# Four interleaved attention layers on one core: projections of every layer staged through HBM, wider exponentials in the last layer, zeros set later

## The chip, the core and the metric

The kernel runs on one core of a Trainium2 chip. The core has five engines with instruction queues of their own: TensorE (PE, matrix multiplies; PEld is its weight load), VectorE (DVE), ScalarE (ACT), GpSimd (POOL) and SyncE (SP), which here only issues transfers. They meet at semaphores. The metric is the time of one execution in device microseconds; the number to beat is the median of seven runs of the kernel before.

## The reference

Four attention layers follow each other on a sequence of 2048 positions with 640 features, 32 heads of 20 features, all in bf16. Layers 0 and 2 use weights A and a sliding window of 256 keys; layers 1 and 3 use weights B and see all keys.

```
def block(x, wqkv, wo, windowed):
    q, k, v = heads(layernorm(x) @ wqkv)             # 32 heads of 20
    s = (q @ k.T) * 20 ** -0.5
    if windowed: s = where(0 <= i - j < 256, s, -1e9)
    return x + merge(softmax(s) @ v) @ wo
x = block(x, A..., True);  x = block(x, B..., False)
x = block(x, A..., True);  x = block(x, B..., False)
```

No maximum is subtracted in the kernel: it exponentiates the scores, and a column of ones beside V gives the sum to divide by.

## The kernel before

**Tiling.** Queries go in chunks of 512 (`c`, four of them), heads in groups of four (`g`, eight). One `Unit` is a layer, a chunk and a group. A score "bank" holds 128 keys by 512 queries of one head, one of the eight PSUM banks. A full unit has 64 banks (16 key blocks, 4 heads), a windowed one 12. There are 4096 full and 768 windowed banks in all. The four heads of a group lie in four strips of 32 partitions, of which 20 hold data and 12 hold zeros, so that the score matmuls (L889) of different heads run side by side.

**The order.** One Python loop (L866) writes the whole program in order, one "tick" for each tile of three banks (of two for every other tile in the early stage). A tick issues the score matmuls of its tile (L889), the exponential over it on ACT (L903), then side work, then for windowed tiles the mask product on DVE (L935), and last the value matmuls of a tile two or three ticks older (L953), which add up in PSUM bank 7. Score tiles alternate between banks 0 to 2 and 3 to 5; bank 6 (early also 5) is left for the side work. Units of neighbouring layers are interleaved: the first parts of layer 1 run between the windowed units of layer 0, layer 2's windowed units between the units of layer 1 (later 3). The last 24 units are layer 3, chunks 1 to 3, with nothing beside them but their own output projections.

**Side work.** Layer norm (`t_ln`), value, key and query projections (`t_v`, `t_qk_window`, `t_full`), output projection (`t_out`) and the normalization of a finished unit (`t_tail`) are generators in a list sorted by the unit that needs them. `pump` (L220) runs them for as much credit as `rate` (L849) gives the tick: 1.2 before the first full unit, later a value that spreads the work before its due time, at least 0.33 in the last layer; one credit is about 4.5 matmuls of a projection. `chain` gives the early path of layer 0 into layer 1 a lead of five units. `require` runs tasks regardless of credit when a unit cannot be written without them. `keep_clock` (L578) adds matmuls without use (L588) where the side work of the last three ticks is small; it is on from the first full unit up to layer 3, chunk 1.

**Projections.** In layers 1 and 3, `t_full` makes a block of 128 of the 640 columns of K or Q (five matmuls of 128x512), evacuates it into a staging tile (`st`, four of them) and stores it in HBM (`k_d`, `q_d`). `load_unit` (L671) brings a unit's values, keys and queries back: one transfer for V and eight for Q and K, one per strip, all on SP's queue. `load_ahead` issues the next full unit's loads once its blocks are written and buffers are free. In layers 0 and 2, `t_qk_window` makes K and Q of one group directly in SBUF with weights padded from 80 to 128 columns, so each chunk needs eight pairs in place of five. The padded weights are built in layer 0, chunk 0 (`get_w`, L304), kept in HBM (`wqk_d`) and loaded again by later chunks. `cap` lets three query tiles (`qa`) live, so this work can run only three units ahead. Stores of K, Q and V are issued by SP, too.

**The start.** DVE clears `wop`, `kts` and `qts` (L118) and makes small constants (L128 to L139) before the first layer-norm statistics (L356). SP loads the input and the weights meanwhile.

The lines of evacuation are shared: L281 is ACT's copy, L283 DVE's; before the first full unit ACT does them, afterwards DVE.

Of the kernel before, what the change touches and what calls it, by code (L numbers as in the profile page):

```python
# [26 lines left out]
HD = D // 2  # L27
VW = DH + 1

PARTS = {  # L30
# [6 lines left out]
def kernel(  # L37
# [18 lines left out]
    big = pool("big", 1)  # L56
    wqkp = pool("wqkp", 9)
    kvp = pool("kvp", 3)
    qap = pool("qap", 3)
    kap = pool("kap", 18)  # L60
    vap = pool("vap", 10)
# [29 lines left out]
    kts = [big.tile([P, S], BF16, name=f"kt{n}", tag=f"kt{n}") for n in range(3)]  # L91
    qts = [big.tile([P, C], BF16, name=f"qt{n}", tag=f"qt{n}") for n in range(4)]

    ps = psp.tile([P, 8, C], F32, name="ps", tag="ps")
    op = ps[:, 7, :]


    wqk_d = dram.tile([G, P, 2 * KD * P], BF16, name="wqk_d", tag="wqk_d")
    k_d = {l: dram.tile([D, S], BF16, name=f"k_d{l}", tag=f"k_d{l}") for l in (1, 3)}
    q_d = {l: dram.tile([NC, D, C], BF16, name=f"q_d{l}", tag=f"q_d{l}") for l in (1, 3)}  # L100
    v_d = {l: dram.tile([P, G, NT * 4 * VW], BF16, name=f"v_d{l}", tag=f"v_d{l}") for l in (1, 3)}

# [13 lines left out]

    for t in (wop, *kts, *qts):
        nc.vector.memset(t[:], 0.0)  # L118
    nc.gpsimd.memset(ident[:], 0.0)
# [6 lines left out]
    def other_constants():  # L126
        load_wop(0)
        nc.vector.memset(op, 0.0)  # L128
# [48 lines left out]
    def push(name, gen, need, left):  # L177
        lead = 0
        if type(name) is tuple and need <= first_use(1, NC - 1, 0):

            chain = {"out": True, "ln": name[1] == 1, "v": name[1] == 1 and name[-1] == 0}
            chain["k"] = chain["q"] = name[-1] == 0
            lead = 5 * chain.get(name[0], False)
        insort(todo, Task(name, gen, need, left, lead))
# [77 lines left out]
    live = Counter()  # L262
    cap = {"qa": 3, "ka": 18, "va": 10, "xnT": 5, "kt": 3, "vt": 3, "qt": 4, "ln": 1, "w": 4, "vs": 2}

# [26 lines left out]
    def get_w(l, n, c, i):  # L291

        t = wqkp.tile([P, KD, P], BF16, name="wqk", tag="wqk")
        wtick[l, n, c, i] = state["tick"] + 4
        if l % 2:
            a = n * D + i * P
            nc.sync.dma_start(out=t[:], in_=wq_view[1][:, :, a : a + P])
            return t
        d = wqk_d[i][:, n * KD * P : (n + 1) * KD * P]
        if l == 0 and c == 0:  # L300
            tv = t[:].rearrange("p c (j m) -> p c j m", j=4)
            nc.gpsimd.memset(tv[:, :, :, DH:32], 0.0)
            src = raw[:, :, n * D + 80 * i : n * D + 80 * (i + 1)]
            nc.vector.tensor_copy(  # L304
                out=tv[:, :, :, 0:DH], in_=src.rearrange("p c (j e) -> p c j e", j=4)
            )
            nc.sync.dma_start(out=d, in_=t[:].rearrange("p c m -> p (c m)"))
            wtick[l, n, c, i] = 0
        else:
            nc.sync.dma_start(out=t[:].rearrange("p c m -> p (c m)"), in_=d)  # L310
        return t
# [48 lines left out]
    def t_ln(l, c):  # L360
# [3 lines left out]
        for n in (1, 0):  # L364
            order = worder[l, n]
            if order and not any(e in wtiles for e in order):
                wtiles[order[0]] = get_w(*order[0])
        users[l, c] = (9, 12, 9, 11)[l]
        mv = mvs.pop((l, c))
# [35 lines left out]
    def t_v(l, c, halves):  # L405
# [41 lines left out]
        for h in halves:  # L447
            if not windowed:
                nc.sync.dma_start(
                    out=v_d[l][:, 4 * h : 4 * h + 4, c * 16 * VW : (c + 1) * 16 * VW],  # L450
                    in_=vs[h][:].rearrange("p g i e -> p g (i e)"),
                )
                live["vs"] -= 1
            ready.add(("v", l, c, h))
# [8 lines left out]

    def t_qk_window(l, c, g):
        while ("xnT", l, c) not in ready:
            yield ("wait", 1)
        yield from room("qa", "ka", "w", "w")
        wt = yield from take_w(l, 0, c, g)
        q = qap.tile([P, C], BF16, name="qa", tag="qa")
        yield from project(wt, xnT[l, c], lambda: q[:])  # L470
        wt = yield from take_w(l, 1, c, g)
        k = kap.tile([P, C], BF16, name="ka", tag="ka")
        yield from project(wt, xnT[l, c], lambda: k[:])
        live["w"] -= 2
        qa[c, g], ka[c, g] = q, k
        used(l, c)
        ready.add(("qk", l, c, g))

    def t_full(l, n, c, b):

# [6 lines left out]
        dst = k_d[l][rows, c * C : (c + 1) * C] if n else q_d[l][c, rows, :]  # L487
        nc.sync.dma_start(out=dst, in_=staging.pop())
        live["w"] -= 1
# [66 lines left out]
    def push_layer(l, c):  # L556
# [3 lines left out]
        if l % 2:  # L560
            halves = ((0,), (1,)) if l == 1 else ((0, 1),)
            for h in halves:
                push(("v", l, c, *h), t_v(l, c, h), need[4 * h[0]], 2.8 * len(h))
            for b in range(KD):
                g = b * P // 80
                for n in (1, 0):
                    worder[l, n].append((l, n, c, b))
                    first = need[g] if n else index[l, c, g, PARTS[l][0] if c == 0 else None]
                    push(("qk"[n], l, c, b), t_full(l, n, c, b), first, 1.1)
            return  # L570
        for g in range(G):
            for n in (0, 1):
                worder[l, n].append((l, n, c, g))
            push(("qk", l, c, g), t_qk_window(l, c, g), need[g], 2.2)
            if g == 0:
                push(("v", l, c), t_v(l, c, (0, 1)), need[0], 5.6)
# [83 lines left out]
    units += [Unit(3, c, g) for c in range(1, NC) for g in range(G)]  # L660
    full = [u for u in units if not u.windowed]
    place = {id(u): n for n, u in enumerate(full)}
    index = {(u.l, u.c, u.g, u.part): n for n, u in enumerate(units)}

    def first_use(l, c, g):
# [3 lines left out]
        return next(index[l, 0, g, p] for p in PARTS[l] if 4 * c < p[1])  # L669

    def load_unit(u):  # L671

        l, c, g = u.l, u.c, u.g
        key = (l, c, g)
        k0, k1 = key_blocks(l, u.part)
        live["vt"] += 1
# [6 lines left out]
        live["qt"] += 1  # L683
        kt[key] = kts[len(loaded) % 3]
        qt[key] = qts[len(loaded) % 4]
        for j in range(4):
# [6 lines left out]
    def unit_needs(u):  # L693
        l, c, g = u.l, u.c, u.g
        if u.windowed:
            return [("qk", l, c, g)]
        k0, k1 = key_blocks(l, u.part)
        chunks = range(k0 // 4, k1 // 4)
        blocks = range(80 * g // P, (80 * g + 79) // P + 1)
        return [("q", l, c, b) for b in blocks] + [  # L700
            n
# [6 lines left out]
    def ensure_loaded(u, force):  # L708
# [6 lines left out]
        elif any(n not in ready for n in needs) or any(  # L715
            live[t] >= cap[t] for t in ("kt", "vt", "qt")
        ):
            return
# [3 lines left out]
    def start_unit(u):  # L722
        for n in unit_needs(u):
            require(n)
        if not u.windowed:
            ensure_loaded(u, True)

    def load_ahead():

        for u in full:  # L730
            if id(u) not in loaded:
                ensure_loaded(u, False)
                return

# [28 lines left out]
    def s_emitted(u):  # L763
        if u.windowed:
            live["qa"] -= 1
            live["ka"] -= (u.c > 0) + (u.c == NC - 1)
        else:
# [9 lines left out]
    def t_tail(l, c, g, on, oT):  # L777
# [38 lines left out]
        if g == G - 1:  # L816
            need = first_use(l + 1, c, 0) if l < 3 else len(units) + c
            push(("out", l, c), t_out(l, c), need, 9.0)
            if l < 3:
                push_layer(l + 1, c)  # L820
    def t_stats0(c):
        for i in range(4):
# [4 lines left out]
    with tc.manual_schedule():  # L827
        other_constants()
        push("stats", t_stats0(0), 0, 0.4)
        push_layer(0, 0)  # L830
        require(("qk", 0, 0, 0))

# [8 lines left out]
        n = 0  # L841
        while n < len(banks):
            size = 2 if len(tiles) % 2 and narrow(banks[n][0]) else 3
            for b in banks[n : n + size]:
                starts.setdefault(id(b[0]), len(tiles))
            tiles.append(banks[n : n + size])
            n += size

        def rate(t):  # L849

            u = tiles[t][0][0]
            if index[u.l, u.c, u.g, u.part] < woven:
# [7 lines left out]

        last_tick[0] = state["tick"] + len(tiles) - 40
        work = deque(maxlen=3)
        started = set()
        pts = deque()
        pushed = set()
        for t in range(len(tiles) + 8):  # L866
            state["tick"] += 1
            n_b = 0
            if t < len(tiles):
                cur = tiles[t]  # L870
                n_b = len(cur)
                for b in cur:
                    u = b[0]
                    if id(u) not in started:
# [9 lines left out]
                        start_unit(u)  # L884
                sp = ps[:, 0:3, :] if t % 2 == 0 else ps[:, 3:6, :]
                for n in range(2):
# [6 lines left out]
                for b in cur:  # L893
                    if b[-1]:
                        s_emitted(b[0])
                pt = ptp.tile([P, 3, C], BF16, name="pt", tag="pt")
                i = 0
# [21 lines left out]
                state["heat"] = 0.0  # L919
            else:  # L920
                pump(2.0, 2.0)

            if 0 < t <= len(tiles):
                cur_, pt_ = masked
                i = 0
                while i < len(cur_):
# [12 lines left out]
                    i = k  # L939
            if n_b:  # L940
                masked = (cur, pt)

# [54 lines left out]
```

The softmax here doesn't subtract the row's maximum and nothing guards it: scores larger than these inputs give would overflow.

## Time and profile before

| | |
|---|---|
| median of 7 runs | 2438.05 us (2423.5 to 2439.68) |
| profiled execution | 2438.93 us, span 2437.2 us |
| busy | PE 2012.9, ACT 2234.8, DVE 871.3, POOL 39.7 us |
| exponentials (L903) | 1704, 2199.0 us |
| projections of K and Q (L337) | 956 matmuls recorded |
| matmuls without use (L588) | 562 |
| granted TensorE clock, mean | 0.829 of full speed |

The profile lists, for each engine, busy time and idle time with the instruction that ended it. Its views used here are: busy time by stretch of the span (columns: stretch, its length, then busy microseconds and instructions of each engine, the granted clock, the share of DMA time and the rate), the waits of one engine (columns: who waited for whom, total, times, longest), and the instructions in order of time (columns: start, duration, engine, line, operation, tiles, count, and the idle time before with its releaser). Matmuls are pipelined and their ends are modelled, so a PE that reads as busy may still have room.

### The profile page before, as it was taken

The page shows a single profiled execution, that of the slowest core. Times are in us where ns is not written, and L with a number is a line of the kernel's source. Part 1 is how long each engine was busy: PE and PEld are TensorE (multiplying, and loading weights), DVE is VectorE, ACT ScalarE, POOL GpSimd, SP SyncE. Part 2 cuts the span into 40 slices and gives each one's busy share as a digit, 9 for nine tenths or more (in the row PEclk, how much of TensorE's full clock was granted, in tenths as well). Part 3 has the DMA queues.
Part 4 walks back from the last instruction along what each step waited for, and adds up shares of the span by engine and source line. Part 5 has one row for each costly group of instructions (what it writes and reads, how often), then busy time and mean ns, then how long its engine had stood idle before and what let it go on. Part 6 is the DMA issues. An engine that isn't in the chain of part 4 may idle for free.

```text
span 2437.2 us, 38778 instructions
## 1 busy us (share of the span) xinstructions
PE 2012.9 (83%) x15662; PEld 741.5 (30%) x15811; DVE 871.3 (36%) x1966; ACT 2234.8 (92%) x1779; POOL 39.7 (2%) x112
## 2 busy tenths in 40 slices
PE   6889889888888898888888898888777777777777
PEld 2334333323322333323322333332222222222222
DVE  6767767423333244433353434542200010001001
ACT  5778888899899999999998999999999999999997
POOL 1000000000000000000000000000000000000000
PEclk9899999987999999989997999999755575557556
DMA  4213223222100122102320032122100010011100
GB/s 146 60 41 82 65 63 91 56 73 74 47 24 26 39 61 80 41 13 55 82 67 16 16 89 75 31 46 63 57 28 26 25 36 26 25 35 31 34 13 12
DMA packets 141124, 120.19 MB, mean 49 GB/s; under 512 B 66064, under 2 KB 129680, under 8 KB 140944
## 3 DMA queue, kind: packets, MB, share of 16 engines
q1 hardware_dynamic: 140944, 117.70, 18.3%
q8 instruction: 124, 2.03, 0.3%
q14 instruction: 56, 0.46, 0.1%
HBM read 96.40 MB, written 21.23 MB: 48 GB/s over the span
## 4 chain that ended last, share of the span: by engine, by line
ACT 43%; PE 31%; issue 14%; DVE 10%; DMA 1%; SPq 0%; POOL 0%; ACTq 0%; DVEq 0%
ACT pt L903 43%; PE ps L337 7%; PE ps L889 7%; PE ps L953 5%; PE ps L510 4%; DVE pt L935 3%; PE ps L588 3%; PE ps L428 3%; DVE oT L760 1%; PE ps L392 1%; DVE on L810 1%; DVE st L283 1%; DVE qa L283 1%; DVE ka L283 1%; PE ps L806 1%
## 5 line engine op out<-in xcount | busy, mean ns | idle before, releaser
L903 ACT ACTIVATE pt<-ps 128x1536 bf16<-128x1536 f32 (+2 forms) x1704 | 2199.0, 1511 | 153.6 <-PE ps L889 130.3
L889 PE MATMUL ps<-qt,kt 32*128 32x512 bf16 x4096 | 667.7, 464 | 260.0 <-ACT pt L903 245.6
L953 PE MATMUL ps<-pt,vt 128*21 128x512 bf16 x4096 | 490.8, 466 | 13.0 <-DVE oT L760 8.0
L889 PEld LDWEIGHTS <-kt 32*128 32x128 bf16 x4096 | 201.2, 94 | 676.9 <-issue 654.2
L935 DVE TENSOR_TENSOR pt<-pt,masks 128x1024 bf16<-128x1024 bf16 (+5 forms) x403 | 240.2, 625 | 165.1 <-ACT pt L903 164.5
L337 PE MATMUL ps<-xnT,wqk 128*128 128x512 bf16 x956 | 271.2, 398 | 25.2 <-issue 5.3
L760 DVE CAST oT<-ps 128x512 bf16<-128x512 f32 x112 | 76.8, 685 | 388.6 <-PE ps L953 388.5
L953 PEld LDWEIGHTS <-vt 128*21 128x21 bf16 x4096 | 106.0, 90 | 326.2 <-issue 315.7
L588 PE MATMUL ps<-masks,ident 128*128 128x512 bf16 x562 | 181.9, 420 | 19.0 <-issue 6.3
L510 PE MATMUL ps<-wop,on 128*128 128x320 bf16 x968 | 174.6, 322 | 5.5 <-DVE x_sb L519 4.2
L810 DVE TENSOR_TENSOR on<-oT,ps 128x512 bf16<-128x512 bf16 x128 | 87.7, 685 | 153.0 <-PE ps L806 148.8
L889 PE MATMUL ps<-qa,ka 32*128 32x384 bf16 (+2 forms) x1408 | 118.8, 279 | 26.9 <-ACT pt L903 23.8
L519 DVE TENSOR_TENSOR x_sb<-x_sb,ps 128x320 bf16<-128x320 bf16 x120 | 58.0, 483 | 219.3 <-PE ps L510 219.1
L337 PEld LDWEIGHTS <-wqk 128*128 128x128 bf16 x1040 | 89.8, 100 | 141.1 <-issue 70.5
L428 PE MATMUL ps<-wv,xnT 128*128 128x320 bf16 x640 | 109.6, 303 | 4.3 <-DVE va L283 1.0
L510 PEld LDWEIGHTS <-on 128*128 128x128 bf16 x968 | 90.0, 103 | 74.0 <-issue 39.2
L953 PE MATMUL ps<-pt,va 128*21 128x384 bf16 (+2 forms) x1408 | 79.3, 292 | 22.1 <-DVE oT L760 16.0
L283 DVE CAST st<-ps 128x512 bf16<-128x512 f32 x78 | 53.8, 690 | 114.4 <-PE ps L337 106.6
L588 PEld LDWEIGHTS <-ident 128*128 128x128 bf16 x627 | 55.9, 103 | 98.6 <-issue 69.1
L799 DVE COPY rT<-ps 32x128 bf16<-32x128 bf16 x128 | 26.9, 210 | 146.9 <-PE ps L797 146.3
L787 DVE RECIPROCAL rz<-ps 128x16 f32<-128x16 f32 x128 | 32.7, 255 | 114.4 <-PE ps L782 113.4
L889 PEld LDWEIGHTS <-ka 32*128 32x128 bf16 x1408 | 40.1, 92 | 96.9 <-issue 91.6
(59 smaller groups left out, 779.8 us busy)
## 6 DMA issues: line engine op xcount, KB each, us to landing
wqk<-wqk_d SPq DMA_DIRECT2D x112, 160.0 KB
vt<-v_d SPq DMA_DIRECT2D x48, 336.0 KB
kt<-k_d SPq DMA_DIRECT2D x192, 80.0 KB
wqk<-in_B_wqkv_dram SPq DMA_DIRECT2D x80, 160.0 KB
qt<-q_d SPq DMA_DIRECT2D x384, 20.0 KB
v_d<-vs SPq DMA_DIRECT2D x16, 336.0 KB
k_d<-st SPq DMA_DIRECT2D x40, 128.0 KB
q_d<-st SPq DMA_DIRECT2D x40, 128.0 KB
```

What stands on the lines that cost most here:

```text
L283: nc.vector.tensor_copy(out=out_, in_=in_)
L337: nc.tensor.matmul(pq, lhsT=wt[:, dc, :], rhs=xt[:, dc, :], start=(dc == 0), stop=(dc == KD - 1),)
L428: nc.tensor.matmul(pv, lhsT=xt[:, dc, i * P : (i + 1) * P], rhs=wv_sb[l % 2][:, dc, h * HD : (h + 1) * HD], start=(dc == 0), stop=(dc == K ...
L510: nc.tensor.matmul(yp, lhsT=on[:, g, qb * P : (qb + 1) * P], rhs=wop[:, g, i * HD : (i + 1) * HD], start=(last or g == 0), stop=(g == G - 1),)
L519: nc.vector.tensor_tensor(out=xv, in0=had, in1=yp, op=ALU.add)
L588: nc.tensor.matmul(ps[:, b, :], lhsT=ident[:], rhs=masks[:, 0, :], start=True, stop=True)
L760: nc.vector.tensor_copy(out=oT[:], in_=op)
L810: nc.vector.tensor_tensor(out=on[:, g, :], in0=oT[:], in1=zb, op=ALU.mult)
L889: nc.tensor.matmul(sp[:, i, col * P : (col + qn) * P], lhsT=u.k(kc, j), rhs=u.q(j, q0, qn), start=True, stop=True,)
L903: nc.scalar.activation(out=pt[:, i:k, b0 * P :], in_=sp[:, i:k, b0 * P :], func=ACT.Exp, scale=SCALE,)
L935: nc.vector.tensor_tensor(out=pt_[:, i:k, b0 * P :], in0=pt_[:, i:k, b0 * P :], in1=mv_, op=ALU.mult,)
L953: nc.tensor.matmul(op[32 * j : 32 * j + VW, q0 * P : (q0 + qn) * P], lhsT=u.v(kc, j), rhs=pt[:, i, col * P : (col + qn) * P], start=(first ...
```

## The change

Five things change.

- **K and Q of layers 0 and 2** go through HBM as those of layers 1 and 3 do, in five unpadded blocks each (`t_block`), except for layer 0, chunk 0, which keeps the padded form (`t_qk_first`). `wqk_d` goes, its weights come from the input in blocks of 128 columns. A windowed unit now has eight loads (20 KB each) in `load_unit`, issued ahead by `load_ahead` from a second list of units. Query tiles `qa` are four in place of three; `qa` and `ka` become fixed tiles, handed out from lists.
- **All stores of K, Q and V** are issued by GpSimd in place of SP.
- **Exponentials of the last 24 units**: an odd tile takes four banks (3 to 6, 2048 columns) where no tail is running, bank 6 is free and no task is awake; else three. Its output goes into the old key tiles.
- **Zeros** of `wop`, `kts`, `qts` and now also of ten key tiles are set by a task (`t_zeros`) that is due at unit 5; the small constants and the masks come after the first layer norm.
- **Pace in the last 24 units**: `rate` is 0.9, and the third step of every tail waits one tick rather than two (`last_tick`).

```diff
+    k_d = {l: dram.tile([D, S], BF16, ...) for l in range(4)}
-    for t in (wop, *kts, *qts):
-        nc.vector.memset(t[:], 0.0)
-        if l % 2:
+        if l or c:
             a = n * D + i * P
-            nc.sync.dma_start(out=t[:], in_=wq_view[1][:, :, a : a + P])
+            nc.sync.dma_start(out=t[:], in_=wq_view[l % 2][:, :, a : a + P])
...
-        nc.sync.dma_start(out=dst, in_=staging.pop())
+        nc.gpsimd.dma_start(out=dst, in_=staging.pop())
...
+        if u.windowed:
+            ka[c, g], qa[c, g] = ka_free.popleft(), qa_free.popleft()
+            for j in range(4):
+                nc.sync.dma_start(out=qa[c, g][strip, :], in_=q_d[l][c, rows, :])
+                nc.sync.dma_start(
+                    out=ka[c, g][strip, :], in_=k_d[l][rows, c * C : (c + 1) * C]
+                )
+            return
...
+        for order in (full, small_units):
+            while order and id(order[0]) in loaded:
+                order.popleft()
+            if order:
+                ensure_loaded(order[0], False)
...
+    def t_zeros():
+        nc.vector.memset(ka_all[:, G:KA, :], 0.0)
+        ready.add("kas")
+        yield ("pe", 0.1)
+        nc.vector.memset(wop[:], 0.0)
+        load_wop(0)
+        yield ("pe", 0.1)
+        for t in (*kts, *qts):
+            nc.vector.memset(t[:], 0.0)
+            yield ("pe", 0.1)
+        ready.add("kts")
...
+            size = 3
+            if t % 2 and not tails and state["held"] is None and mfree[6][0] <= state["tick"]:
+                if all(task.wake > state["tick"] for task in todo):
+                    size = 4
...
+            if t >= len(tiles):
+                return 0.9
...
-                sp = ps[:, 0:3, :] if t % 2 == 0 else ps[:, 3:6, :]
+                sp = ps[:, 0:3, :] if t % 2 == 0 else ps[:, 3:7, :]
```

## The prediction

> **What bounds the kernel now.** I read the busy time by stretch first, cut where the program changes character: start, layer 0 before the first full unit, layer 0 beside layer 1, layers 1 to 3 interleaved, the last 24 units, the end.
>
> ```profile
> core 0: us, PE busy (x) PEld busy (x) DVE busy (x) ACT busy (x) POOL busy (x), PEclk, DMA share, GB/s
> 0.00:25.00 25.00, 7.15 (x36) 3.54 (x36) 14.80 (x34) 5.03 (x7) 8.33 (x31) 1.00 0.91 279
> 25.00:165.00 140.00, 119.37 (x1079) 54.63 (x1087) 99.99 (x247) 110.02 (x155) 9.03 (x23) 0.91 0.16 47
> 165.00:480.00 315.00, 282.49 (x2487) 116.25 (x2520) 211.68 (x453) 262.07 (x221) 7.71 (x18) 0.97 0.28 71
> 480.00:1735.00 1255.00, 1059.59 (x8603) 403.32 (x8704) 473.81 (x1050) 1183.53 (x895) 14.62 (x40) 0.93 0.21 52
> 1735.00:2424.00 689.00, 538.70 (x3444) 161.76 (x3441) 65.59 (x169) 671.88 (x500) 0.00 (x0) 0.57 0.09 27
> ```
>
> ACT is full in the last stage (671.9 of 689) and nearly full in the middle (1183.5 of 1255). From 25 to 480 it is not: 372 of 455, with PE at 402. ACT's waits, in the second, third, fourth and fifth stretch, say for whom:
>
> ```profile
> ACT pt L903 <- PE ps L889: 9.8, 11, 2.6
> ACT ka L281 <- PE ps L337: 6.2, 10, 1.6
> ACT qa L281 <- PE ps L337: 5.7, 9, 1.6
> ...
> ACT pt L903 <- PE ps L889: 41.4, 69, 3.0
> ACT pt L903 <- PE ps L806: 6.1, 1, 6.1
> ...
> ACT pt L903 <- PE ps L889: 61.9, 87, 1.9
> ...
> ACT pt L903 <- PE ps L889: 18.5, 18, 1.5
> ```
>
> It waits for score matmuls that stand behind side work in PE's order. So PE's side work costs time up to 480 us, some of it up to 1735, and at the end only the exponentials count. The one long wait (6.1) is a round trip through HBM, in order of time:
>
> ```profile
> 163.06 0.33 SPq L488 DMA_DIRECT2D q_d<-st  x1
> ...
> 166.57 0.31 SPq L689 DMA_DIRECT2D qt<-q_d  x1
> ...
> 168.54 1.25 PE L889 MATMUL ps<-qt,kt 32*128 32x512 bf16 x2 [4.29 <-DMA kt<-k_d]
> ```
>
> The first full unit's Q was stored at 163.06, its load issued 3.5 us later, and PE stood 4.3 us.
>
> **The change, part by part.**
>
> *Start.* DVE clears from 1.40 to 7.9 (wop 2.19, three kt at 0.91, four qt at 0.27 us) and makes constants until 9.1; the statistics follow at 9.14 and end at 13.2. Now they can begin when the chunk's rows land: 0.66 MB at the 224 to 364 GB/s of the stretches from 2 us on, so about 4.5 us, ending near 8.7. But the copy of the first weights (L304) stands before the next layer-norm step on DVE, and `raw` (1.6 MB more, 2.3 MB in all) lands at about 10 us by the same rates. So the path gains about 14.65 - 11.3 = 3.3 us, not 4.5. The zeros come back: 6.0 us as before plus ten key tiles, the size of wop, 2.19 us; 8.2 us on DVE, all written in one tick or two since each step takes 0.1 credit, near 43 us, where DVE is 8.6 of 10 busy. Queued behind them are the mask products, and value matmuls behind those; these are three ticks late by design, about 4 us of cover at 1.9 us a tick (140 us for some 72 ticks). What sticks out is 8.2 - 4 = 4, less some idle DVE: +3. **Start and zeros: 0** (bounds -4 and +6). Without the cover it would be +5. `load_wop` moves past the weights on SP; its first reader is at 106 us, so it costs nothing.
>
> *The stall at 163 us.* The path into layer 1 runs out(0,0), layer norm, V, K, Q, store, load. Output matmuls took from about 104 to 134 us, since the padded projections of chunk 1 could run only three units ahead and were forced, 2.2 credits per unit, in the 4.8 ticks of a windowed unit: of 5.8 credits 2.9 were left for the path, so 9 credits took 15 ticks. After the change chunk 1's K and Q cost 11 credits in place of 17.6 and have no such limit: with 1.2 a tick, chunk 0's 15.4, zeros, tails and chunk 1's 18.6 are done by about tick 36 of 38. The path then gets about 5 credits a unit and ends some ten ticks earlier than its unit. The 6.1 us wait goes. **-6** (0 to -8). Next late would be chunk 2's norm, hidden by its later due time.
>
> *Layer 0, chunks 1 to 3.* Each drops six projections of 30 matmuls. A projection is 1.25 us with its drain (five matmuls, "x5 1.25"), 1.08 pitch: 18 x 1.08 = 19.4 us of PE, and 18 evacuations of 0.59 (ACT) or 0.69 us (DVE). ACT's waits on PE here are 25 + 48 us, so not all PE time is path; I take half: **-10** (0 to -20). The weights' 256-byte rows are those of layer 1 (same 160 KB load, 80 times in this trace; one 1.7 us wait).
>
> *Layer 2.* 24 projections, 26 us of PE, 16.6 us of DVE. ACT waits 62 us here, and `keep_clock` (508 of its matmuls in this stretch) fills quiet ticks again, so only crowded ticks gain. The 26 us are about a tenth of the side work: **-6** (+5 to -15).
>
> *Loads.* 56 windowed units x 8 issues x 0.37 us (start to start at 168) = 166 us of SP, less 42 weight loads and 16 stores. In layer 0 that is 3 us a unit beside 3.4 of a full one and the 17 us they last together. SP's order matters more: a load now waits there for its store to land, and weight loads queue behind it; a late one stops PE (1.7 us above). Due times leave 16 ticks, about 21 us, against a round trip of 5.5, so these hide in the main case.
>
> *Stores on GpSimd.* 166 of them; no row here shows one, and POOL is 2% busy. Behind a store that waits for its evacuation stand `rstd` and the ones of V, whose readers come two ticks later. The nearest row, SP's issue, is 0.33 us. The Trainium skill speaks against the move (*SBUF — State Buffer*, "A bandwidth-pool intuition that's wrong"): GpSimd writes the descriptors itself and is locked out while VectorE holds the shared port; a 0.62 us transfer became 3.1 us. By the row the move costs nothing, by the rule up to 2.5 us for each exposed round trip. DVE's work here is mostly reads of PSUM and mask products, so I take about 1 us each, on three, for loads and stores together: **+3** (-2 to +15).
>
> *Wide exponentials.* In the last stage score matmuls of successive tiles start at 1871.04, 1872.39, 1873.73: 1.343 us a tile. The one- and two- and three-bank exponentials alone last about 0.59, 1.02 and 1.45 us, 0.83 ns a column, so 1536 columns are 1.28 us and a tile's own cost is 0.063 us. A tail blocks six ticks, 18 banks; the other 46 go 3.5 a tick: 19.1 ticks for 21.3. With 21 units at 2.2 and three with an output projection at 0.9, 49 exponentials fewer: 49 x 0.063 = -3. The skill's rule (*ScalarE: Activation LUTs*, "Rules for kernel authors") budgets about 0.3 us an ACTIVATE: -15. The row decides, since ACT runs these back to back and overlaps the fixed part. *Pace 0.9*: an output projection took 4 to 5 us of ACT idle when spread; the one at the end already runs at 0.9, and there ticks take 1.7 us against 1.34 (2408.30, 2409.68, then 2411.70, 2413.40), about 5 in all. +0.5 each, three times. **Last stage: -1.5** (-8 to +6).
>
> Sum: 0 - 6 - 10 - 6 + 3 - 1.5 = -20.5. From the profiled 2438.9 us that is **2418.4**; the median of the runs, 2438.05, is 0.9 lower, so I say 2418.
>
> **The rivals.**
>
> *PE sets the pace up to 480 us*: all of 19.4 and 12 of layer 2 count, and the stall goes: 0 - 7 - 19 - 12 + 2 - 2 = -38, **2400**. For it: PE is 402 of 455 busy at nearly full clock. Against: DVE has 312 too, and its masks and tails remain.
>
> *Hidden anyway*: freed ticks fill with other side work and with L588, and the zeros stick out; only the stall and 3 us of exponentials go, +5 from zeros and stores: **2434**. For it: rate is fixed at 1.2 before 165 us, whatever is left to do.
>
> *Slower: windowed loads arrive late.* Where a windowed unit's K and Q are finished just before it, `require` issues load behind store and PE stands as at 163 us: 6.1 us of ACT. The gain is gone at 20.5 / 6.1 = 3.4 such units of 56; ten give 2438.9 - 20.5 + 61 = **2479**. The place is layer 0's chunks 2 and 3, where the path's lead of five units outranks them, and where one query tile of four must be free. For it: 4.3 us of PE wait once already; against: only 4.9 us of such waits over 96 loaded units.
>
> **How the numbers follow.** Main case 0.50, own range 2405 to 2431; PE-paced 0.20; hidden 0.12; late loads 0.18, of which half end above 2450. Two runs of this kernel can be told apart by about 0.3%, 7.3 us: faster is below 2430.7, which takes nearly all of the first two and a bit of the third and fourth: 0.72. Same, to 2445.4, is most of the hidden case: 0.10. Slower 0.18. The range, 2390 to 2450, leaves out a tenth at either end: the bounds of the parts below, the worse late loads above.
>
> **What would show it.** First exponential near 22 us (25.25 before). No L903 wait of 6 us near 160. L337 matmuls down from 1040 weight loads to 830. ACT's waits on L889 up to 480 us down by some 15. L903 with a 2048-column form, about 140 to 150 of it at a pace of 1.77 us. DMA waits at L889 for `ka` and `qa` below 10 us in sum; above 30, the slower rival holds. POOL's order late (DVE waiting for `rstd` or for `st`) would price the stores. I am wrong if the tiles of the last stage pace differently, or if the waits of ACT on PE stay at 120 us though the projections are gone.

## The result, and the profile after

The change made the kernel slower: 2448.61 us median of 13 runs (2441.39 to 2460.05), against 2435.96 us for the kernel before in runs on the same chip. The ratio is 1.0057, with a 95% interval of 1.004 to 1.0073, so some 14 us are lost where I had forecast a gain of 20. (The ratio is that of a kernel's time to the time of the kernel before in runs beside it.) The profiled execution took 2442.72 us, with a span of 2440.7.

Busy time by stretch of the changed kernel, with the cuts used for the kernel before:

```profile
core 0: us, PE busy (x) PEld busy (x) DVE busy (x) ACT busy (x) POOL busy (x), PEclk, DMA share, GB/s
0.00:25.00 25.00, 9.12 (x43) 4.19 (x44) 9.85 (x26) 6.57 (x9) 8.65 (x32) 1.00 0.70 236
25.00:165.00 140.00, 114.49 (x1002) 52.94 (x1009) 99.50 (x241) 100.68 (x147) 15.21 (x34) 0.88 0.23 53
165.00:480.00 315.00, 270.85 (x2369) 107.84 (x2392) 193.70 (x417) 252.00 (x221) 36.07 (x68) 0.93 0.27 73
480.00:1735.00 1255.00, 1048.06 (x8667) 407.92 (x8773) 469.24 (x1047) 1188.98 (x904) 73.36 (x144) 0.95 0.23 59
1735.00:2424.00 689.00, 525.92 (x3489) 157.50 (x3488) 67.66 (x175) 677.45 (x459) 0.00 (x0) 0.55 0.09 27
```

ACT does less in the second and third stretch (100.7 and 252.0 us, where it was 110.0 and 262.1), though PE has fewer projections to do. Its waits for score matmuls in the second to the fifth stretch, in this order (L968 is the exponential now, L950 the score matmul):

```profile
ACT pt L968 <- PE ps L950: 20.2, 18, 9.7
...
ACT pt L968 <- PE ps L950: 58.7, 59, 10.4
...
ACT pt L968 <- PE ps L950: 60.5, 88, 1.8
...
ACT pt L968 <- PE ps L950: 10.8, 21, 1.1
```

Up to 480 us they grew from 51 to 79 us, and each of the first two stretches has one wait of about 10 us that the kernel before didn't have. In the last stage they fell from 18.5 to 10.8.

To see where time is lost, I took for each kernel the time at which it had exponentiated as many columns as the kernel before had at a given time. The difference (a plus is late) is the loss so far, whatever the order of the side work:

```
time of the kernel before    50    98   170   242   362   402   480  1763  2426
changed kernel              -2.1  +9.9 +15.2 +18.9 +17.2 +25.7 +21.5 +11.3  +3.3
```

The changed kernel loses 24 us between 50 and 480 us: 12 by 98, 9 more by 242, 8.5 between 362 and 402. At 480 us the side work left to do is the same in both but for the smaller projections of layer 2, so this is a loss and not work done early. Afterwards it gains in the last stage (8 us from 1763 on). Between 480 and 880 us single executions differ though the work is the same: the changed kernel makes up 12 us on the kernel before there, at a granted clock of 0.95, and the run with zeros on GpSimd, told of below, whose order of work is the same from tick 25 on, makes up 3, at 0.90. So I compare traces up to 480 us and in the last stage only, and whole kernels by their ratios.

Three places stand out. The first is the **zeros**, in order of time:

```profile
48.96 2.19 DVE L845 MEMSET ka<- 128x2560 uint32 x1 [0.48 <-issue]
51.63 2.19 DVE L848 MEMSET wop<- 128x2560 uint32 x1 [0.48 <-issue]
...
57.94 0.67 DVE L779 CAST oT<-ps 128x512 bf16<-128x512 f32 x1
58.66 0.61 PE L1018 MATMUL ps<-pt,va 128*21 128x384 bf16 x8 [10.11 <-DVE oT L779]
59.62 1.30 ACT L968 ACTIVATE pt<-ps 128x256 bf16<-128x256 f32 x2 [9.72 <-PE ps L950]
```

All memsets come in one burst from 48.96 on. The copy of the finished unit's output (L779) stands behind the large ones; it frees PSUM bank 7, and the next unit's value matmuls wait for it 10.11 us. The score matmuls stand behind these on PE, so ACT waits 9.72 us.

The zeros are not all of this stop. In the six traces below that have no such burst, PE still waits 5.0 us for the same copy. From the run with zeros on GpSimd, VectorE's last statistics of chunk 1, the copy, and PE behind it:

```profile
50.97 0.21 DVE L352 BATCH_NORM_AGGREGATE mv<-stats 128x2 f32<-128x12 f32 x1
...
51.52 0.68 DVE L779 CAST oT<-ps 128x512 bf16<-128x512 f32 x1
...
52.25 0.61 PE L1018 MATMUL ps<-pt,va 128*21 128x384 bf16 x8 [5.01 <-DVE oT L779]
```

The four statistics of chunk 1 take VectorE some 4 us there, from 47.09 on, and stand where the burst stood. In the order of the program they come at tick 19, just before the copy; in the kernel before they come at tick 15, and PE has no wait of that length for this copy. With four query tiles in place of three, the program of the kernel before would have them at tick 19 as well, which points to the fourth tile. No run tested it, and what it costs is not known: the kernel before has a stop of PE of 3.4 us of another kind at nearly the same place.

The second is the **first full unit**:

```profile
177.33 0.46 SPq L693 DMA_DIRECT2D vt<-v_d  x1
177.49 2.32 PE L331 MATMUL ps<-xnT,wqk 128*128 128x512 bf16 x9 [0.59 <-DMA ka<-k_d]
180.83 1.07 POOL L485 DMA_DIRECT2D q_d<-st  x2 [0.54 <-DVE st L282]
182.84 0.30 SPq L705 DMA_DIRECT2D qt<-q_d  x1
184.96 1.96 PE L950 MATMUL ps<-qt,kt 32*128 32x512 bf16 x3 [5.15 <-DMA kt<-k_d]
186.96 2.37 ACT L968 ACTIVATE pt<-ps 128x1536 bf16<-128x1536 f32 x2 [10.35 <-PE ps L950]
```

The wait of 6.10 us at 163 us did not go, it became 10.35 us: projections run at 177.49, a store follows at 180.83, the load at 182.84, and PE resumes at 184.96.

The third is a **weight tile** that comes late:

```profile
386.27 0.32 SPq L686 DMA_DIRECT2D ka<-k_d  x1
386.64 1.77 SPq L296 DMA_DIRECT2D wqk<-in_B_wqkv_dram  x3
...
391.55 2.12 PE L331 MATMUL ps<-xnT,wqk 128*128 128x512 bf16 x5 [2.62 <-DMA wqk<-in_B_wqkv_dram]
394.81 2.37 ACT L968 ACTIVATE pt<-ps 128x1536 bf16<-128x1536 f32 x2 [4.58 <-PE ps L950]
```

Its issue stands on SP behind a run of 17 issues of a full and a windowed unit from 380.2 on. Between 95 and 480 us, weights stopped PE for 1.7 us before the change (first line) and for 11.7 after it:

```profile
PE ps L337 <- DMA wqk<-in_B_wqkv_dram: 1.7, 1, 1.7
...
PE ps L331 <- DMA wqk<-in_A_wqkv_dram: 6.1, 4, 2.5
PE ps L331 <- DMA wqk<-in_B_wqkv_dram: 5.6, 4, 2.6
```

A stop can cost more than its own length, because the granted clock falls behind it. Stretches of 4 us around the second place, columns as above:

```profile
176.00:180.00 4.00, 3.15 (x25) 1.39 (x26) 2.05 (x6) 0.61 (x2) 0.25 (x1) 1.00 0.58 152
180.00:184.00 4.00, 0.00 (x0) 0.00 (x0) 1.14 (x2) 0.00 (x0) 1.90 (x4) 0.95 0.39 134
184.00:188.00 4.00, 2.69 (x6) 0.54 (x7) 0.00 (x0) 1.04 (x1) 0.00 (x0) 0.50 0.38 91
188.00:192.00 4.00, 4.00 (x22) 1.16 (x20) 0.90 (x2) 2.39 (x3) 0.54 (x1) 0.70 0.77 164
192.00:196.00 4.00, 3.11 (x32) 1.28 (x32) 2.26 (x4) 2.86 (x3) 0.54 (x1) 1.00 0.32 105
```

PE stands 5.15 us, up to 184.96; the clock is 0.50 in the 4 us after 184, 0.70 in the next 4, and full from 192 us on. In those 8 us PE gets 4.8 us' worth of clock, so the stop of 5 us costs it about 8 (an estimate from these rows). A projection's five matmuls take 2.31 us at the low clock (at 187.66) and 1.25 at the full one. The Trainium skill has the rule for this (*TensorE: Matmul & The Clock Gate*, "Part 1: The HAM clock gate"): half clock after an idle window of about 3.4 us, full clock again after as long a time of work. This trace agrees in kind.

### The profile page after: what moved, and what is told of

It reads as the page before. It is cut to its first block, busy times and chain, and to the rows that moved or that the text cites. A ratio compares the mean times of both kernels' runs of the same rounds, so it can differ in the third digit from the quotient of the medians.

```text
span 2440.7 us, 39182 instructions
## 1 busy us (share of the span) xinstructions
PE 1975.2 (81%) x15603; PEld 733.0 (30%) x15747; DVE 845.4 (35%) x1918; ACT 2231.2 (91%) x1739; POOL 133.3 (5%) x278
## 2 busy tenths in 40 slices
DMA packets 170823, 129.07 MB, mean 53 GB/s; under 512 B 115536, under 2 KB 153296, under 8 KB 170640
## 4 chain that ended last, share of the span: by engine, by line
ACT 43%; PE 21%; issue 14%; DVE 5%; DMA 1%; SPq 1%; ACTq 0%; POOL 0%; DVEq 0%; POOLq 0%
ACT pt L968 36%; ACT ka L968 7%; PE ps L950 5%; PE ps L507 3%; PE ps L1018 3%; PE ps L589 3%; PE ps L331 3%; PE ps L422 2%; DVE pt L1001 1%; DVE st L282 1%; DMA wqk<-in_B_wqkv_dram 1%; PE ps L386 1%; DVE oT L779 1%; PE ps L538 0%; DVE x_sb L516 0%
## 5 line engine op out<-in xcount | busy, mean ns | idle before, releaser
L968 ACT ACTIVATE pt<-ps 128x1536 bf16<-128x1536 f32 (+5 forms) x1517 | 1997.4, 1485 | 162.0 <-PE ps L950 151.3
L950 PE MATMUL ps<-qt,kt 32*128 32x512 bf16 x4096 | 645.8, 465 | 292.4 <-ACT pt L968 173.1
L1018 PE MATMUL ps<-pt,vt 128*21 128x512 bf16 x3536 | 470.4, 447 | 18.4 <-DVE oT L779 11.7
L950 PEld LDWEIGHTS <-kt 32*128 32x128 bf16 x4096 | 198.3, 94 | 688.5 <-issue 662.5
L968 ACT ACTIVATE ka<-ps 128x2048 bf16<-128x2048 f32 x140 | 298.5, 2132 | 0.0
L331 PE MATMUL ps<-xnT,wqk 128*128 128x512 bf16 x768 | 217.6, 398 | 29.6 <-DMA wqk<-in_B_wqkv_dram 6.6
L779 DVE CAST oT<-ps 128x512 bf16<-128x512 f32 x112 | 76.7, 685 | 460.9 <-PE ps L1018 460.8
L589 PE MATMUL ps<-masks,ident 128*128 128x512 bf16 x691 | 220.1, 414 | 14.3 <-issue 5.9
L282 DVE CAST st<-ps 128x512 bf16<-128x512 f32 x133 | 91.8, 690 | 209.6 <-PE ps L331 209.4
L1018 PE MATMUL ps<-ka,vt 128*21 128x512 bf16 x560 | 147.9, 598 | 0.0
L950 PE MATMUL ps<-qa,ka 32*128 32x384 bf16 (+2 forms) x1408 | 119.4, 283 | 32.3 <-ACT pt L968 27.6
L331 PEld LDWEIGHTS <-wqk 128*128 128x128 bf16 x830 | 71.5, 100 | 123.3 <-issue 52.8
L589 PEld LDWEIGHTS <-ident 128*128 128x128 bf16 x773 | 68.2, 102 | 114.4 <-issue 76.2
```

What stands on the lines that cost most here:

```text
L282: nc.vector.tensor_copy(out=out_, in_=in_)
L331: nc.tensor.matmul(pq, lhsT=wt[:, dc, :], rhs=xt[:, dc, :], start=(dc == 0), stop=(dc == KD - 1),)
L589: nc.tensor.matmul(ps[:, b, :], lhsT=ident[:], rhs=masks[:, 0, :], start=True, stop=True)
L779: nc.vector.tensor_copy(out=oT[:], in_=op)
L950: nc.tensor.matmul(sp[:, i, col * P : (col + qn) * P], lhsT=u.k(kc, j), rhs=u.q(j, q0, qn), start=True, stop=True,)
L968: nc.scalar.activation(out=pt[:, i:k, b0 * P :], in_=sp[:, i:k, b0 * P :], func=ACT.Exp, scale=SCALE,)
```

## The experiments

My theory at first was: the zeros' burst, and SP's order (loads that wait there for stores, weights behind them), both in layer 0. The rivals: the wide tiles or GpSimd's stores do the harm; or the projections' new path costs time by which work is done when. The first two sets look at one part of the change each.

**Zeros back at the start.** On VectorE, where the kernel before has them.

```
+    for t in (wop, *kts, *qts):
+        nc.vector.memset(t[:], 0.0)
+    nc.vector.memset(ka_all[:, G:KA, :], 0.0)
...
-        push("zeros", t_zeros(), index[0, 0, 5, None], 1.2)
```

> Only the zeros move back to the start of the program, on VectorE; all else is the changed kernel. Theory (the zeros written in one tick at 48 to 59 us hold the copy that frees the bank of the value matmuls, about 10 us of ScalarE's idle time there, and SP's order costs the rest): 2443 us, that is 6 less than the changed kernel, since about 8 come back near 50 us and 2 are paid again at the start. Rival (the zeros are hidden, and the loss up to 400 us is that of the projections' new path alone): 2450, the 2 of the start added and nothing gained.

Measured: 2444.53 us, ratio 1.0047 (1.0025 to 1.0069). The median moved towards the theory, by 2.4 us instead of 6, but the intervals overlap. In the trace ACT's wait of 9.72 us falls to 4.64, that behind the statistics, and the loss at 98 us is still 7.4.

**Zeros on GpSimd.** The better test of the burst: it stays background work, in another place.

```
-        nc.vector.memset(wop[:], 0.0)
+        nc.gpsimd.memset(wop[:], 0.0)
         load_wop(0)
-        yield ("pe", 0.1)
+        yield ("wait", 2)
```

(and the same for the other tiles)

> The changed kernel with the zeros set by GpSimd, two ticks apart, in place of VectorE in one tick. Theory (VectorE's burst holds the copy that frees the value matmuls' bank): 2445 us, about 4 less than the changed kernel, and no wait of 10 us of ScalarE near 59 us. Rival (GpSimd's memsets are slower and hold up the norm's power and the stores behind them): 2450 or more.

Measured: 2442.54 us, ratio 1.0023 (1.0006 to 1.004), 0.0034 below the changed kernel, 8.3 us. The loss at 98 us falls from 9.9 to 2.0, though ACT still waits 4.63 us behind the statistics. So VectorE's burst costs about 8 by the ratio (the two intervals just touch), twice what I expected even then. GpSimd's memset of the same tile takes 4.36 us in place of 2.19.

**Layer 0 padded.** Layer 0 goes back to padded projections that stay in SBUF; of the edit one place is shown, the weights and loads of layer 0 go with it.

```
-        if l or c:
+        if l:
             for b in range(KD):
```

> Layer 0 alone goes back to padded projections without HBM; layer 2 through HBM, stores on GpSimd, zeros as background work and the wide exponentials stay. Theory (layer 0's way through HBM loses about 15 us up to 400 us, by the queue on SP and the longer wait of the first full unit; layer 2's gains some): 2434 us. Rival (layer 0's projections do save, and the zeros and layer 2 lose the time): 2455 or more.

Measured: 2434.19 us, ratio 0.9994 (0.9978 to 1.001). As the theory had it: the loss of some 15 us comes with layer 0's way through HBM, and layer 2's does no harm of that size. The loss at 480 us falls from 21.5 to 3.2. Why layer 0 loses was still open.

**No wide tiles**, and **stores back on SP**:

```
-            if t % 2 and not tails and state["held"] is None and mfree[6][0] <= state["tick"]:
-                if all(task.wake > state["tick"] for task in todo):
-                    size = 4
```

```
-        nc.gpsimd.dma_start(out=dst, in_=staging.pop())
+        nc.sync.dma_start(out=dst, in_=staging.pop())
```

(and the same for V)

> The changed kernel with three banks in every tile of the last layer; its pace of 0.9 there stays. Theory (one exponential fewer in 35 saves 0.063 us each, 49 in all): 2452 us, 3.5 more than the changed kernel. Rival (all of the 9 us that the last stage gains come from the wide tiles): 2458.

> The changed kernel with the stores of K, Q and V back on SP's queue. Theory (the harm is SP's order: loads wait there for stores; with the stores on the same queue a store also stands behind a waiting load): 2454 us, 5 more than the changed kernel, with longer waits for kt and for weights. Rival (GpSimd's queue takes longer from issue to landing, 2.1 us and more, and that is the loss): 2440.

Measured: 2454.82 us, ratio 1.0083 (1.0058 to 1.0109), and 2455.92 us, ratio 1.0077 (1.0047 to 1.0107). Neither is the culprit: each part undone makes the ratio worse, by 6 and 5 us, though these intervals overlap that of the changed kernel. From 1763 us to the end the trace gains 8.0 us with wide tiles and 2.5 without, so they are worth 5.5. A store's issue takes GpSimd 0.54 us and lands 2.1 us later (0.76 and 3.5 for V).

**Loads that keep their distance.** A test of SP's order (`ready.at` holds the tick of a store):

```
-        elif any(n not in ready for n in needs) or any(
+        elif any(
+            n not in ready or state["tick"] < ready.at.get(n, 0) + 4 for n in needs
+        ) or any(
```

> The changed kernel, but a unit's K and Q are asked for ahead of time only when their last store was issued at least four ticks before (some 7 us), so that a load seldom stands on SP waiting for its store with weights behind it. Theory (SP's order costs about 4 us at the first full unit and 6 or more near 390 us): 2441 us, 8 less than the changed kernel, and no wait of PE of over 2 us for weights. Rival (which side work is done when costs the time, not the order of the loads): 2447 to 2450, with the weights' waits gone all the same.

Measured: 2453.54 us, ratio 1.0067 (1.0042 to 1.0092): a miss. The waits for weights went from 11.7 us to 5.4 (those for A from 6.1 to 0.6), but one of 2.8 us was left where the theory had none over 2, and the rule held back full units as well: PE's waits for `kt` rose from 5.3 to 10.0 us, with a new stop of 4.5 us up to 206 us. The wait at the first full unit stayed at 10.3 us. The run trades one late load for another. The largest stop stays when SP's order is changed, so its cause had to be looked for elsewhere.

**The kernel before with the last stage alone**, and **a first combination** (layer 0 padded, zeros on GpSimd, loads at a distance); of the first, against the kernel before, one line:

```
-                sp = ps[:, 0:3, :] if t % 2 == 0 else ps[:, 3:6, :]
+                sp = ps[:, 0:3, :] if t % 2 == 0 else ps[:, 3:7, :]
```

> The kernel before with the change's last stage alone: wide tiles and the pace of 0.9 in the last layer (four query tiles in place of three, and the constants after the first norm, come with it); all projections padded as before, stores on SP, zeros at the start. Theory (the last stage gained 8 to 9 us in the trace, 5.5 of it by the wide tiles): 2428 us. Rival (that gain was a return of earlier losses, and the wide tiles alone are worth 3): 2433.

> Layer 0 padded and without HBM as before the change, zeros on GpSimd two ticks apart, loads only four ticks after their stores; layer 2 through HBM, stores on GpSimd and wide exponentials as changed. Theory (the three losses are separate): 2428 us, some 8 below the kernel before. Rival (what the zeros cost in layer 0 is given back later, and layer 2's loads cost nothing): 2434, as with layer 0 padded alone.

Measured: 2429.73 us, ratio 0.9979 (0.9966 to 0.9993), and 2436.22 us, ratio 0.9992 (0.9973 to 1.0011). The last stage alone is faster than the kernel before, by 5 us. The second, which adds layer 2 through HBM, gains nothing more.

**What holds the first full unit.** I followed the planner's own order, tick by tick, in front of that unit (layer 1's first, at tick 79). A projection must hold one of four weight slots (`cap["w"]`, by `room`) and keeps it while its weights load for four ticks:

```
tick 67  K1, Q1, K2, Q2 of layer 0, chunk 2 (due 20 to 24) hold the four slots
tick 69  layer 1's norm is done: its K0 and Q0 (due 10) may run
tick 72  K0, Q0 look for a slot: none; K1 runs
tick 73  K0, Q0 look: none; K1's end is seen and Q1 runs, each gives its slot back;
         layer 1's K2, Q2 (due 21), next in the list, take both
tick 76  layer 0's K2 runs;  tick 77, 78  layer 1's K2, Q2 run
tick 79  the unit begins; Q0 isn't done, so K0 and Q0 are forced, and the load comes behind them
```

A finished task gives its slot back when the list comes to it again, after the tasks ahead of it have looked, and the next one behind it takes the slot in the same tick. So the K and Q that the next unit needs starve behind work with later due times. In the kernel before, and with layer 0 padded, they run at ticks 76 and 77: there a windowed projection also needs one of three (four) query tiles, and that limit kept layer 0's next chunk from taking all four slots. The change took this limit away. (The due numbers are those by which the list is sorted.)

**The first K and Q without a wait for a slot**, as a test of that:

```
-        yield from room("w")
+        if (l, c, b) == (1, 0, 0):
+            live["w"] += 1
+        else:
+            yield from room("w")
```

> The changed kernel, but the K and the Q that layer 1's first unit needs no longer wait for one of the four weight slots, which the projections of layer 0's third chunk hold; in the order of the program they then come at ticks 72 and 73 in place of 79, and the unit's load at tick 74 in place of 79. Theory (the starved first K and Q are why the stall at the first full unit grew to 10 us, and the clock falls after it): 2440 us, 8 to 9 less than the changed kernel, with no wait of over 3 us for kt. Rival (the projections that then come later pay the same): 2447 to 2450.

Measured: 2429.75 us, ratio 0.9972 (0.9961 to 0.9982), 0.0085 below the changed kernel, 21 us. From the trace of this kernel, in order of time: the first load of the unit's Q on SP, ACT's next exponential that had to wait, and PE and ACT at the next late weight tile (L971 is the exponential here, L953 the score matmul):

```profile
168.96 0.30 SPq L708 DMA_DIRECT2D qt<-q_d  x1
...
176.22 2.37 ACT L971 ACTIVATE pt<-ps 128x1536 bf16<-128x1536 f32 x2 [0.28 <-PE ps L953]
...
191.38 0.61 PE L331 MATMUL ps<-xnT,wqk 128*128 128x512 bf16 x1 [5.51 <-DMA wqk<-in_B_wqkv_dram]
194.87 2.37 ACT L971 ACTIVATE pt<-ps 128x1024 bf16<-128x1024 f32 x2 [7.19 <-PE ps L953]
```

The load goes out 14 us earlier than with the change alone, and from 168 us to 187 ACT waits 0.60 us at the longest: the stop at the first full unit is gone, so the slots were its cause. A late weight tile at 191.38 costs 7.19 us right behind it, though. The edit of two tasks out of some 150 turns the change from a loss into a gain, more than twice what I expected. By 242 us it has won 9 us, about what I expected; 9 more come by 402 us. There the order of the side work differs, too, up to tick 183, and why it is the better one was not followed up.

**Weights on GpSimd's queue:**

```
-            nc.sync.dma_start(out=t[:], in_=wq_view[l % 2][:, :, a : a + P])
+            nc.gpsimd.dma_start(out=t[:], in_=wq_view[l % 2][:, :, a : a + P])
```

> The changed kernel with the weight loads on GpSimd's queue, so that none stands behind a load of K or Q on SP. Theory (12 us of PE's waits for weights between 95 and 480 us, and the lower clock after them, cost about 8 us): 2441 us. Rival (GpSimd issues the 640 pieces of a weight tile slowly and the norm's power and the stores wait behind them): 2450 or more, with the waits for weights still there.

Measured: 2438.87 us, ratio 1.0018 (1.0008 to 1.0028), 0.0039 below the changed kernel, 9.5 us. Two issues on GpSimd in order of time, the table of DMA issues (the last number is the time to landing), and PE's waits for weights between 95 and 480 us:

```profile
169.90 1.74 POOL L296 DMA_DIRECT2D wqk<-in_B_wqkv_dram  x2
```

```profile
wqk<-in_B_wqkv_dram POOLq DMA_DIRECT2D x80, 160.0 KB, 3.9
wqk<-in_A_wqkv_dram POOLq DMA_DIRECT2D x70, 160.0 KB, 3.4
```

```profile
PE ps L331 <- DMA wqk<-in_B_wqkv_dram: 4.4, 3, 2.9
```

With 0.2 for weights A, the waits fall from 11.7 to 4.6 us. The wait at the first full unit stays (12.22 us), as it must if slots cause it. The edit does a second thing, told below: it also cuts the number of packets, so it isn't a pure test of the order.

**All three edits** as shown, and, as another candidate, **the last stage alone with zeros on GpSimd**, for which the key tiles need none:

```
     def t_zeros():
-        nc.gpsimd.memset(ka_all[:, G:KA, :], 0.0)
         ready.add("kas")
```

> The changed kernel with three edits: zeros on GpSimd two ticks apart, the first K and Q of layer 1 without a wait for a slot, weights on GpSimd's queue. Theory (the three causes are separate and add up: 8 for the zeros as measured, 8 and 8): 2425 us, below the kernel before. Rival (they share the same lost time, up to 400 us): 2436.

> The kernel before with the change's last stage alone, as in the earlier run, and the zeros of the output weights, key and query tiles on GpSimd as background work; no zeros for the windowed keys, which nothing needs here. Theory (the start pays 4 to 5 us for the zeros, and GpSimd's are hidden): 2425 us. Rival (what the start gains is lost before the first full unit): 2430.

Measured: 2413.94 us, ratio 0.9912 (0.9895 to 0.9928), and 2432.88 us, ratio 0.9998 (0.9985 to 1.0012). The first is the fastest of all. Apart, its edits lower the ratio by 0.0034 + 0.0085 + 0.0039 = 0.0158; together by 0.0145. So the three add up, in the main, and together they make up for more than the loss of 0.0057. They are not the loss alone: they also take away what the kernel before has, its stop of 6.1 us at the first full unit and the small packets of weights B. What they would do to the kernel before was not tested. The stretches of the fastest kernel:

```profile
0.00:25.00 25.00, 9.14 (x52) 4.49 (x52) 10.04 (x27) 6.91 (x10) 8.65 (x32) 1.00 0.70 236
25.00:165.00 140.00, 118.60 (x1047) 55.17 (x1056) 98.05 (x240) 105.58 (x152) 50.74 (x67) 0.89 0.22 58
165.00:480.00 315.00, 281.75 (x2531) 115.78 (x2561) 206.62 (x445) 273.97 (x236) 77.79 (x118) 0.98 0.30 81
```

ACT's work from 165 to 480 us is 274.0 us, where it was 252.0 with the change alone and 262.1 before. The second candidate is 4.5 us ahead of the earlier run with the last stage alone at 50 us and 3.3 behind it at 98, for a reason of its own, told at the end.

How far each kernel is behind the kernel before (us, as above):

```
time of the kernel before        50    98   170   242   362   402   480
changed kernel                 -2.1  +9.9 +15.2 +18.9 +17.2 +25.7 +21.5
zeros on GpSimd                -3.4  +2.0  +6.2 +12.2  +9.3 +18.2 +14.0
first K and Q without a wait   -5.6 +11.2  +7.1  +9.9  +4.2  +8.0  +3.8
weights on GpSimd              -4.5 +10.9 +18.5 +19.0 +13.9 +19.6 +15.4
all three                      -3.3  +3.7  +1.6  -3.7 -10.6  -7.2 -11.5
```

At 480 us the three alone win 7.5, 17.7 and 6.1 us, 31.3 in sum; together they win 33.0.

## Why the prediction was wrong, step by step

The direction was wrong; the time lies in the range (2390 to 2450), but at its upper edge. With the three edits the change gives 21 us. That this is close to the sum of 20.5 is luck: the shares are others, and part of the gain is no part of the change.

*Start and zeros, 0.* The start was read about right. The first exponential comes at 23.45 us here, 1.8 earlier than before, but at 20.4 to 23.5 in the eleven traces without zeros at the start, 22.2 on average: 3 us earlier, where I had 3.3. The zeros were mis-sized: +3, measured 8.3. The step that failed is "these are three ticks late by design, about 4 us of cover". The first value matmuls of a new unit have no such cover, since they need bank 7, and the copy that frees it stood behind the zeros. I had named the mask products as what is queued behind the memsets, and missed this copy. I also put nothing on the fourth query tile, which by the order of the program moves chunk 1's statistics in front of the same copy; PE waits 5.0 us behind them where the burst is gone.

*The stall at 163 us, -6.* The failed step is "Chunk 1's K and Q cost 11 credits in place of 17.6 and have no such limit". I booked the end of the limit as a gain. It was what kept layer 0's next chunk out of the weight slots, and without it layer 1's first K and Q starved: the wait grew from 6.1 to 10.35 us where I had it gone, and letting the first K and Q pass is worth 21 us in the measured ratio. A second reading was wrong as well: "Output matmuls took from about 104 to 134 us". They ran from 119 to 134, and in the changed kernel from 128 to 144. Their first line in both, the kernel before first:

```profile
119.12 1.25 PE L510 MATMUL ps<-wop,on 128*128 128x320 bf16 x8 [0.34 <-DVE on L810]
...
128.51 1.25 PE L507 MATMUL ps<-wop,on 128*128 128x320 bf16 x8 [0.66 <-DVE on L832]
```

Both wait for the last head group of chunk 0 to be normalized (`on`). So the path's start was set by that tail, not by credits, and more credits couldn't bring it forward. The spare credits before it went to chunk 2's norm and V.

*Layer 0, chunks 1 to 3, -10.* The projections went (830 weight loads, as forecast). Their gain isn't measured alone. With the three edits the kernel is 11.5 us ahead at 480 us, of which 3.3 were there at 50; the other 8 hold the stop of 6.1 us as well, so no size for this term follows.

*Layer 2, -6 (+5 to -15).* The last stage alone has 0.9979, and with layer 2 through HBM (layer 0 padded, zeros on GpSimd, loads at a distance) 0.9992; the intervals overlap. No gain shows. `keep_clock`, which I named, may have taken the freed ticks: 691 of its matmuls were recorded, 562 before.

*Loads and stores, +3 (-2 to +15).* The stores on GpSimd cost nothing that can be seen, so the row was right, and the lockout that the Trainium skill warns of (*SBUF — State Buffer*, "A bandwidth-pool intuition that's wrong") did not show on them: an issue took 0.54 to 0.75 us in all 150 stores of K and Q. The term was mis-sized on the other side: "weight loads queue behind it; a late one stops PE (1.7 us above)" named the place, and 9.5 us is what the weights' move gives back, by the order or by the fewer packets told of below. I priced one such stop at its own length. Waits for `qa` and `ka` stayed small, so the slower rival as I put it, windowed loads that arrive late, is not what happened, and its test (below 10 us in sum) was passed.

*Last stage, -1.5.* The mechanism was right, both sizes were small:

```profile
L968 ACT ACTIVATE ka<-ps 128x2048 bf16<-128x2048 f32 x140 | 298.5, 2132 | 0.0
```

140 wide exponentials, 1657 exponentials in all in place of 1704. Away from the output projections the trace gains about 0.2 us per 36 us, 3.6 over the stage, and without wide tiles it gains 5.5 less. This answers to the 3 from 0.063 us each, or to twice that, and not to the 15 by the price that the skill states (*ScalarE: Activation LUTs*, "Rules for kernel authors"). The output projections, for which I took 0.5 us of loss each, gained as well, 4 to 5 us in sum. Alone, this stage gives 5 us.

Behind the single terms stands one omission: I priced every stop of PE at its length. By the rows above, the low clock after the stop of 5.15 us takes another 3.2 us of PE's work.

## What to carry to other kernels

A limit that seems only to hold work back may also keep that work from taking something that more urgent work needs; before removing it, list what the freed tasks will hold, and who asks for the same. When a queue of background work has slots, see that a slot that comes free goes to the first in need. Price a stop of PE with the slow clock behind it. And look behind a burst on an engine for the one short copy that frees a bank.

## What the runs showed of the hardware

**A small cast on VectorE took 6.81 us** in the kernel with the last stage alone and zeros on GpSimd:

```profile
57.10 6.81 DVE L815 CAST hl<-rz 128x16 bf16<-128x16 f32 x1
...
57.52 5.30 POOL L853 MEMSET kt<- 128x2048 bf16 x3
```

Elsewhere in this trace the cast of 16 elements per partition takes 0.17 us. It began with GpSimd's memset of a weight tile, just ahead of those of the key tiles, and ended at 63.91, when three key tiles and two query tiles were cleared, and the kernel lost 7 us between 62 and 74. In the changed kernel with zeros on GpSimd the same cast, at the same place, took 0.43 us, in the fastest one 0.76, and 1.85 in the tail after it. The Trainium skill states a lock of this kind (*SBUF — State Buffer*, "Who interferes with whom": VectorE and GpSimd share a pair of ports, and one waits for the other's whole instruction). That fits in part: here the cast outlasted a whole row of memsets, not one instruction, and which form of VectorE instruction is caught wasn't tested. So zeros on GpSimd are a risk, and 8 us is what they gave here.

**Weights loaded by GpSimd go in fewer packets.** With the weights on its queue the whole program has 82,025 DMA packets in place of 170,823, and 19,536 under 512 bytes in place of 115,536, for the same 160 KB per load; 150 loads account for 96,000 fewer small ones, 640 each, and for some 64 larger ones each. An issue takes GpSimd 0.86 us, on SP 0.37 at the least. How much of the 9.5 us is due to this and how much to the order wasn't told apart.

**Still open**: between 74 and 98 us every other trace loses 4 to 8 us against that of the kernel before, those with layer 0 padded included, and the cause is not known. The changed kernel loses 8 us between 1376 and 1456 us, at a granted clock of 0.87 where the kernel before has 0.98, with the same side work but for layer 2's projections. The others with layer 2 through HBM lose 4 to 9 there; of the two without, one loses nothing and one 4. No run was made on it. What layer 0's fewer projections are worth by themselves was not measured either.
